# An own list scheduler for two interleaved attention layers: order, buffers and copying engine set by a planned-time simulation

## The chip, the cores and the metric

The kernel runs on one core of a Trainium2 chip. The core has five engines that matter here: PE (TensorE, matrix products; its weight loads are listed apart as PEld), DVE (VectorE), ACT (ScalarE), POOL (GpSimd) and SP (SyncE, which here only issues DMAs). Each executes its own list of instructions strictly in the order in which they stand in it, and waits on semaphores for the others. The metric is the time of one execution on the device, in microseconds (us); the lower the better.

## What is computed

Four residual layers over a sequence of 2048 rows of 576 numbers: A, B, A, B, with the same weights in both turns.

```
x = x + A(layernorm(x));  x = x + B(layernorm(x))     (twice)

A: q, k, v of 32 heads x 18; each position attends to itself and 7 earlier ones,
   2 apart (8 logits, softmax); output projection
B: for each segment of 32 rows, in order:
     h = [mem (8 rows), segment (32 rows)]
     q, k, v = h Wq, h Wk, h Wv            32 heads x 128
     p = softmax(mask(q k^T / sqrt(128)))  40 x 40 per head
     o = (p v) Wo;  mem = o[0:8];  output rows = o[8:40]
```

In B the memory of a segment is computed from the one before: 64 segments that follow one another, twice. A is local.

## The kernel before

All values are kept transposed, features on the 128 partitions (576 is 4.5 blocks of 128). Matrix operands are bf16, sums are f32 in PSUM, which has eight banks: three single ones in rotation (`ps_r`), one tile of four banks (`ps_o`), one for the output projection (`ps_y`).

Both B layers run together: a step t handles segment t of layer 2 (lane 0) and segment t - 6 of layer 4 (lane 1), 80 columns in all: twice 32 rows and twice 8 rows of memory. There are 64 + 6 = 70 steps. `b_step` (L638) issues a step:

- `qk` (L441, 11 groups of three heads): 30 matmuls of 80 columns into one bank, then one copy to `b_qk`, in turn by ACT (L459) and DVE (L461).
- `vpass` (L470): three passes of two halves, 20 matmuls each, for the rows of lane 0, of the memory, and of lane 1. Copies by ACT (L487) or DVE (L489) as written in the step.
- `score_m`, `score_x`: the logits of the memory rows and of the segment rows, for 16 heads at a time (r = 0, 1). `softmax` (L492): maximum, subtraction (DVE), exp (ACT), sum, reciprocal (DVE), multiplication by DVE for the memory rows (`em`) and by POOL for the segment rows (`ex`, L503); DVE transposes both (L521, L543).
- `pv_m` (L545, per r): the memory rows' product with V into the four-bank tile, copied to `OT` by DVE (L560). `pv_x` (L563): the segment rows' product, copied to `OT` by ACT and DVE in turn (L588, L590).
- `oproj` (L593): 160 matmuls into `b_psY`; it needs the memory columns of `OT` from this step and the segment columns from the step before. `mem_out` (L604): three DVE copies put the new memory into the next step's input `hT` (L616 to L618). With these the next step's q, k and v can start.

The A layers go in tiles of 64 rows (32 tiles a layer), `a_tile` (L247): layer norm, q, k, v from 15 weight blocks that SP streams from DRAM through six buffers (`a_w`, L242), products q*k on POOL (`a_big`, L310), logits by a matmul, softmax, spreading back into the four-bank tile (`a_psB`), copies to `a_big` by ACT and DVE in turn (L350, L352), multiplication with v on DVE (L363), three reductions on POOL (L364, L365, L367), output projection from five more blocks, second layer norm. The last 14 columns of k and v go to the next tile through `a_halo` by DVE copies (L284, L285, L299, L300). `finish_out` (L396) adds the last layer and writes the output.

What sets the order: the step's instructions are issued at high priority in the order written in `b_step`; the tiles are generators, which `fill` (L662) advances by a planned amount of PE time after each block. `chain` fixes the order of the matmul blocks on PE. The other engines' order is set by a scheduler from priorities.

## Time and profile before

| | us |
|---|---|
| median of 3 runs | 3577.89 (3569.14 to 3592.28) |
| profiled execution, own time | 3581.54 |
| its span, first to last instruction | 3579.8 |
| PE busy | 2646.4 (74%) |
| DVE busy | 1583.8 (44%) |
| ACT busy | 1051.7 (29%) |
| POOL busy | 1007.2 (28%) |
| mean granted clock of PE | 0.880 |

Busy time is that in which at least one instruction of the engine was at work. The granted clock says at what share of its full speed PE was allowed to run. In the groups of instructions a row gives line, engine, operation, tiles and count, then busy time and the mean of one in ns, then the engine's idle time just before them with what ended it. In a timeline a row begins with start and length in us, and has in brackets how long the engine had been idle and what released it. In the windows, a row is: stretch, length, then busy time and count for PE, PEld, DVE, ACT, POOL, then granted clock, DMA share and GB/s.

### The profile page before, as it was taken

The numbers are of one execution on the slowest core, as the hardware profiler recorded it, in microseconds if no ns is written. First come the engines' busy times: TensorE is split into PE (matmuls) and PEld (weight loads), VectorE is DVE, ScalarE is ACT, GpSimd is POOL, SyncE is SP. The second block draws the span as 40 slices with busy tenths as digits, with TensorE's granted clock in tenths as the row PEclk, the third lists the DMA queues.
The fourth block names the chain that finished last, engine by engine and source line by source line (L and its number), as shares of the span: only waits on it lengthen the run. The fifth ranks groups of instructions, "written<-read, shape, count | busy, mean of one in ns | idle before, by whom it ended". The sixth has DMA issues, their size and how long they took to land. (4 is left out here: it accounts for less than half of the span.)

```text
span 3579.8 us, 159066 instructions
## 1 busy us (share of the span) xinstructions
PE 2646.4 (74%) x73360; PEld 2213.0 (62%) x73360; DVE 1583.8 (44%) x3949; ACT 1051.7 (29%) x2317; POOL 1007.2 (28%) x1007
## 2 busy tenths in 40 slices
PE   0577777777768868777786786777688687778888
PEld 0466666666656646665665665666566466657667
DVE  1344444444444434443453454444445344444443
ACT  0233232232323323322332332333233233222232
POOL 3233323323232322323323332233323323221210
PEclk9998889898979879897897988989899799978899
DMA  9233223232232323223332332333323333222210
GB/s 288 76 85 88 77 78 84 80 97 70 83 84 74 97 84 93 80 85 88 85 99 66 89 95 68 98 88 86 85 73 97 91 86 84 82 68 59 56 40 12
DMA packets 368640, 304.06 MB, mean 85 GB/s; under 512 B 146788, under 2 KB 364452, under 8 KB 366436
## 3 DMA queue, kind: packets, MB, share of 16 engines
q1 hardware_dynamic: 364724, 275.02, 27.7%
q0 software_dynamic: 3248, 18.88, 1.5%
q8 instruction: 573, 9.39, 1.1%
q14 instruction: 95, 0.78, 0.1%
HBM read 260.88 MB, written 32.90 MB: 82 GB/s over the span
## 5 line engine op out<-in xcount | busy, mean ns | idle before, releaser
L452 PE MATMUL b_psqk<-hT,wq 128*128 128x80 bf16 x8960 | 729.9, 209 | 171.6 <-DVE b_qk L461 69.0
L452 PE MATMUL b_psqk<-hT,wk 128*128 128x80 bf16 x8960 | 729.0, 209 | 0.0
L601 PE MATMUL b_psY<-OT,wo 128*128 128x80 bf16 (+1 forms) x11360 | 551.8, 222 | 182.0 <-DVE OT L560 181.2
L601 PEld LDWEIGHTS <-wo 128*128 128x128 bf16 x11360 | 532.6, 114 | 187.8 <-issue 185.0
L452 PEld LDWEIGHTS <-wq 128*128 128x128 bf16 x8960 | 506.9, 104 | 213.2 <-issue 194.5
L484 PE MATMUL b_psv<-wv,hT 128*32 128x512 bf16 x6720 | 476.1, 405 | 43.7 <-DVE b_qk L461 31.3
L452 PEld LDWEIGHTS <-wk 128*128 128x128 bf16 x8960 | 496.1, 105 | 0.2 <-issue 0.2
L454 PE MATMUL b_psqk<-hT,wq_r 128*128 128x80 bf16 x2240 | 467.5, 209 | 0.1
L454 PE MATMUL b_psqk<-hT,wk_r 128*128 128x80 bf16 x2240 | 467.0, 208 | 0.0
L484 PEld LDWEIGHTS <-hT 128*32 128x32 bf16 x8400 | 219.6, 101 | 271.8 <-issue 98.6
L503 POOL TENSOR_TENSOR ex<-ex,b_sumx 128x384 bf16<-128x384 bf16 x140 | 116.6, 833 | 936.0 <-DVE b_sumx L502 595.1
L459 ACT CAST b_qk<-b_psqk 128x480 bf16<-128x480 f32 (+1 forms) x420 | 223.9, 534 | 491.7 <-PE b_psqk L454 489.7
L310 POOL TENSOR_TENSOR a_big<-a_q,a_k 128x1024 bf16<-128x1024 bf16 (+1 forms) x192 | 320.1, 1692 | 134.6 <-ACT a_k L296 132.8
L290 PE MATMUL a_psqkv<-a_xn,a_w 128*128 128x64 bf16 x4800 | 260.9, 202 | 130.4 <-DMA a_w<-wA_blk 111.5
L461 DVE CAST b_qk<-b_psqk 128x480 bf16<-128x480 f32 x350 | 224.7, 646 | 209.2 <-PE b_psqk L454 207.0
L364 POOL TENSOR_TENSOR a_big<-a_big 128x1280 bf16<-128x1280 bf16 x64 | 166.7, 2605 | 513.3 <-DVE a_big L363 513.3
L290 PEld LDWEIGHTS <-a_w 128*128 128x128 bf16 x4800 | 195.6, 103 | 186.2 <-DMA a_w<-wA_blk 138.7
L487 ACT CAST V<-b_psv 128x512 bf16<-128x512 f32 x350 | 200.9, 588 | 180.7 <-PE b_psv L484 180.3
L454 PEld LDWEIGHTS <-wq_r 128*128 128x128 bf16 x2240 | 234.4, 105 | 0.0
L454 PEld LDWEIGHTS <-wk_r 128*128 128x128 bf16 x2240 | 234.0, 104 | 0.0
L390 POOL TENSOR_TENSOR xnb<-xres,ln_st 128x256 bf16<-128x256 f32 (+1 forms) x128 | 65.7, 533 | 454.8 <-DVE ln_st L232 454.8
L484 PE MATMUL b_psv<-wv_r,hT 128*32 128x512 bf16 x1680 | 175.7, 401 | 2.2 <-issue 2.2
(139 smaller groups left out, 3586.0 us busy)
## 6 DMA issues: line engine op xcount, KB each, us to landing
a_w<-wA_blk SPq DMA_DIRECT2D x1280, 160.0 KB, 3.1
x1T<-xres SPq DMA_DIRECT2D x32, 160.0 KB, 2.8
xres<-x1T SPq DMA_DIRECT2D x32, 160.0 KB, 2.5
d2T<-b_stg SPq DMA_DIRECT2D x64, 80.0 KB, 1.9
dl<-d2T SPq DMA_DIRECT2D x32, 160.0 KB, 2.3
x3T<-xres SPq DMA_DIRECT2D x32, 160.0 KB, 3.1
d4T<-b_stg SPq DMA_DIRECT2D x64, 80.0 KB, 2.4
xres<-x3T SPq DMA_DIRECT2D x32, 160.0 KB, 2.7
```

The source lines that it names most:

```text
L290: mm = [nc.tensor.matmul(ps[:, c, :], lhsT=w[:, kc, :], rhs=xn[:, kc, :], start=(kc == 0), stop=(kc == 4)) for kc in range(5)]
L310: nc.gpsimd.tensor_tensor(out=big[:, c0:c0 + nb], in0=qT[:, c0:c0 + nb].unsqueeze(2).to_broadcast([P, nb, AW, T]), in1=win(kT, c0, nb), op ...
L364: nc.gpsimd.tensor_tensor(out=big[:, :, 0:4], in0=big[:, :, 0:4], in1=big[:, :, 4:8], op=ALU.add)
L390: nc.gpsimd.tensor_tensor(out=o, in0=i, in1=bc(m), op=ALU.subtract)
L452: mm.append(nc.tensor.matmul(ps[:, hh, wi, :], lhsT=wt[:, kc, h * P:(h + 1) * P], rhs=hT[:, kc, 0:W80], start=(kc == 0), stop=False))
L454: mm.append(nc.tensor.matmul(ps[:, hh, wi, :], lhsT=wr[:, (h % 16) * P:(h % 16 + 1) * P], rhs=hT[:, 4 + h // 16, 0:W80], start=False, stop ...
L459: nc.scalar.copy(out=sb[:, 0:n], in_=ps[:, 0:n])
L461: nc.vector.tensor_copy(out=sb[:, 0:n], in_=ps[:, 0:n])
L484: mm.append(nc.tensor.matmul(ps[c * 32:(c + 1) * 32, :], lhsT=l, rhs=w, start=(kc == 0), stop=(kc == 4)))
L487: nc.scalar.copy(out=o, in_=ps[:])
L503: eng.tensor_tensor(out=e, in0=e, in1=ss[:].unsqueeze(len(shp) - 1).to_broadcast(shp), op=ALU.mult)
L601: mm.append(nc.tensor.matmul(self.psY[:, mb, c0:], lhsT=self.wo[:, w0:w0 + P], rhs=self.OT[:, h, c0:], start=(h == 0 and mb == 0), stop=(h ...
```

## The change

All arithmetic stays, and so do matmuls, tilings, the sizes and counts of the buffers (but for one `fin` instead of two, and four instead of three of the small softmax sums), the two lanes and their distance of 6 steps, and the setup. What changes is who decides the order. The program is now first written down as a graph of operations (`_Op`), each with the engine or the engines that may do it, its planned length, a priority (a time in steps), the operations that it depends on, and the buffers that it takes and uses. `_Plan.run` then plays it through in planned time: whenever an engine is free, it takes the ready operation with the lowest priority number whose buffers are free, emits its instructions at once, and frees buffers when the last user is done. So the order of instructions on each of the five engines, the buffer, and the engine for each copy that ACT and DVE can both do come out of this play. The order is emitted as it is (`manual_schedule`). Semaphores are set from the data's dependencies, as before.

Beside this: all PSUM banks in rotation, and all other buffers, are plain tiles handed out by the plan; the halo copies are POOL's; the three reductions can be POOL's or DVE's (`PD`); the copies of q, k, v, `OT`, `big` and of the layer norms' inputs can be ACT's or DVE's (`AD_`); the squares can be DVE's; the projection is cut into eight pieces that other work can come between; V's two halves and both scores are single operations. ACT's copies are written as an activation with scale 1.

The diff, cut to its core:

```diff
+    LAT = {"PE": 0.22, "DVE": 0.1, "ACT": 0.1, "POOL": 0.12, "SP": 2.4, "NONE": 0.0}
+    SWITCH = 0.1
...
+    def run(self, log=None):
+        ready = {e: [] for e in self.LAT}
...
+                for e, heap in ready.items():
+                    if free[e] > now + 1e-9:
+                        continue
+                    skipped = []
+                    pick = None
+                    while heap:
+                        it = heapq.heappop(heap)
+                        o = it[2]
+                        if o.done:
+                            continue
+                        need = {}
+                        for b in o.acq:
+                            need[b.pool] = need.get(b.pool, 0) + 1
+                        if all(len(self.pools[p]) >= k for p, k in need.items()):
+                            pick = o
+                            break
+                        skipped.append(it)
+                    for it in skipped:
+                        heapq.heappush(heap, it)
+                    if pick is None:
+                        continue
+                    o = pick
+                    o.done = True
+                    for b in o.acq:
+                        b.t = self.pools[b.pool].pop(0)
+                    us = o.us[o.eng.index(e)]
+                    if e == "PE":
+                        if o.mode != mode:
+                            us += self.SWITCH
+                            mode = o.mode
+                    if o.fn is not None:
+                        o.fn(e)
+                    busy[e] += us
+                    if log is not None:
+                        log.append((now, us, e, o))
+                    free[e] = now + us
...
+                elif what == "done":
+                    for b in o.uses:
+                        b.left -= 1
+                        if b.left == 0:
+                            self.pools[b.pool].append(b.t)
+                    for s in o.next:
+                        s.wait -= 1
+                        if s.wait == 0:
+                            enable(s, now)
+        return now, busy
...
+def _act(n):
+    return 0.22 + 0.00072 * n
+def _dve(n):
+    return 0.15 + 0.00105 * n
+def _evac(n):
+    return (_act(n), _dve(n))
+AD_ = ("ACT", "DVE")
...
+                    def hcopy(e, part=part):
+                        h = dst[part].t[:, :, 0:HALO]
+                        if first:
+                            nc.gpsimd.memset(h, 0.0)
+                        else:
+                            nc.gpsimd.tensor_copy(out=h, in_=hin[0].t[:, part - 1])
+                    got[part, "h"] = pl.op("POOL", 0.25, hcopy, pr(0.22), [o] if first else [o, hin[1]],
+                                           uses=[dst[part]] if first else [dst[part], hin[0]])
...
+            evs.append(pl.op(AD_, _evac(512),
+                             lambda e, g=g, ps=ps: self.copy(e, big.t[:, 0:4, :, g * 16:(g + 1) * 16],
+                                                             ps.t[:, g, :].rearrange("p (c w t) -> p c w t", c=4, w=AW)),
+                             pr(0.56), [b], uses=[ps, big]))
...
+        PD = ("POOL", "DVE")
+        o = pl.op(PD, (2.6, 0.85), lambda e: self.tt(e, big.t[:, :, 0:4], big.t[:, :, 0:4], big.t[:, :, 4:8], ALU.add),
+                  pr(0.64), mus, uses=[big])
+        o = pl.op(PD, (1.44, 0.5), lambda e: self.tt(e, big.t[:, :, 0:2], big.t[:, :, 0:2], big.t[:, :, 2:4], ALU.add),
+                  pr(0.66), [o], uses=[big])
+        o = o_o = pl.op(PD, (0.78, 0.33), lambda e: self.tt(e, oT.t[:], big.t[:, :, 0], big.t[:, :, 1], ALU.add),
+                        pr(0.68), [o], acq=[oT], uses=[big])
...
+        if r == 0:
+            self.OTm = pl.buf("OTm")
+            self.om_ev = [pl.op(AD_, (0.4, 0.41), lambda e: self.copy(e, o_, ps.t[:, :, 0:64].rearrange("p c (i q) -> p c i q", i=4)),
+                                prio, [o], acq=[self.OTm], uses=[ps])]
+        else:
+            self.om_ev.append(pl.op(AD_, (0.4, 0.41), lambda e: self.copy(e, o_, ps.t[:, :, 0:64].rearrange("p c (i q) -> p c i q", i=4)),
+                                    prio, [o, self.om_ev[0]], uses=[ps, self.OTm]))
...
+        gate = pl.op("NONE", 0.0, None, prio, [o], acq=[OTx])
+        self.OTx = OTx
+        self.ox_ev = []
...
+            self.ox_ev.append(pl.op(AD_, _evac(512), ev, prio, [gate], uses=[ps, OTx]))
...
     def b_step(self, t):
-        self.qkt, self.PTm, newPTx = {}, {}, {}
-        last = t == self.nsteps - 1
-        self.PTx = newPTx
-        seq = []
+        self.qkt, self.qk_ev, self.PT = {}, {}, {}
+        if t == 0:
+            self.vpass(t, 2, 0.0)
         for g in range(11):
-            seq.append((self.qk, t, g))
-            if g == 9:
-                seq.append((self.load_x, t + 1))
-            if g == 6:
-                seq += [(self.vpass, t, 1, ("act", "dve")), (self.score_m, 0), (self.score_x, 0)]
-        seq += [(self.vpass, t, 0, ("act", "act")), (self.score_m, 1), (self.score_x, 1), (self.pv_m, 0),
-                (self.oproj, 0, 12), (self.pv_m, 1), (self.oproj, 12, 16), (self.oproj, 16, 24), (self.oproj, 24, 32),
-                (self.mem_out, t), (self.x_out, t - 1), (self.pv_x,)]
-        if not last:
-            seq.append((self.vpass, t + 1, 2, ("act", "act")))
-        for fn, *args in seq:
-            c0 = self.clk
-            with self.hp():
-                fn(*args)
-            if self.clk > c0:
-                self.fill(SHARE * (self.clk - c0))
...
+            self.qk(t, g, t + 0.05 + 0.045 * g)
+        self.vpass(t, 1, t + 0.36)
+        self.vpass(t, 0, t + 0.54)
+        self.scores(t, 0, "m", t + 0.30)
+        self.scores(t, 0, "x", t + 0.32)
+        self.scores(t, 1, "m", t + 0.51)
+        self.scores(t, 1, "x", t + 0.57)
+        self.pv_m(t, 0, t + 0.60)
+        self.pv_m(t, 1, t + 0.62)
+        dep = self.oproj(t, [t + 0.63 + 0.02 * k for k in range(8)])
+        if t + 1 < self.nsteps:
+            self.load_x(t + 1)
+        self.mem_out(t, dep, t + 0.8)
+        self.x_out(t - 1, dep, t + 0.9)
+        self.pv_x(t, t + 0.92)
+        if t + 1 < self.nsteps:
+            self.vpass(t + 1, 2, t + 0.95)
...
+        with self.tc.manual_schedule():
+            self.setup()
+            self.trace()
...
+        end, busy = pl.run(LOG)
```

PE has the same 73,360 matmuls in the built program. Three places show how the order moves.

DVE before, around the second memory copy to `OT` of a step (L560; `b_ptx` is the transposed `ex`, which POOL multiplies first; L284 and L285 are halo copies):

```order
L560 CAST OT<-b_psom 128x16x16
L503 TENSOR_TENSOR em_262<-em_262,b_summ 128x4x80
L501 TENSOR_REDUCE b_sumx<-ex_264 128x8
L521 STREAM_TRANSPOSE b_ptm<-em_262 128x384
L502 RECIPROCAL b_sumx<-b_sumx 128x8
L285 COPY a_v<-a_halo_47653 128x5x14
L543 STREAM_TRANSPOSE b_ptx<-ex_264 128x512
L284 COPY a_k<-a_halo_47653 128x5x14
L560 CAST OT<-b_psom 128x16x16
L616 CAST hT_259<-b_psY 128x4x16
```

ACT after, at the same place of a step (`xs` is the layer norm's input, `big` and `ex` as before, the copies of 128x16x16 to `OT` are the memory copies, `o` is the four-bank tile):

```order
L223 ACTIVATE xT_303<-r_342 128x320
L223 ACTIVATE big_319<-o_343 128x4x8x16
L673 ACTIVATE ex_273<-r_340 128x8x48
L223 ACTIVATE xs_308<-xT_303 128x5x64
L223 ACTIVATE OT<-o_343 128x16x16
L394 ACTIVATE xs_308<-xT_303 128x5x64
L223 ACTIVATE OT<-o_343 128x16x16
L223 ACTIVATE stg_293<-psY 128x5x2x32
```

The memory copies have moved from DVE, where the transpose of `ex` and the halo stood ahead of them, to ACT, where a copy of `big`, an exp and a layer norm's input stand ahead.

POOL before, around the multiplication of `ex` (L503): reductions of one tile, products of the next.

```order
L364 TENSOR_TENSOR a_big<-a_big 128x5x256
L365 TENSOR_TENSOR a_big<-a_big 128x5x128
L367 TENSOR_TENSOR a_o<-a_big 128x320
L310 TENSOR_TENSOR a_big<-a_q,a_k 128x1024 x2
L503 TENSOR_TENSOR ex_264<-ex_264,b_sumx 128x8x48
L310 TENSOR_TENSOR a_big<-a_q,a_k 128x512
```

POOL after, at a comparable place (L489, L504 and L505 are halo copies, the 128x1024 and 128x512 rows the products):

```order
L489 COPY kT_312<-halo_315 128x5x14
L230 TENSOR_TENSOR big_319<-qT_311,kT_312 128x1024
L489 COPY vT_314<-halo_315 128x5x14
L230 TENSOR_TENSOR big_319<-qT_311,kT_312 128x1024
L230 TENSOR_TENSOR ex_272<-ex_272,sum_299 128x8x48
L504 COPY halo_316<-kT_312 128x70
L505 COPY halo_316<-vT_314 128x70
L230 TENSOR_TENSOR big_319<-qT_311,kT_312 128x512
```

The reductions no longer stand there (DVE has them in this tile), the halo copies do, and two of the three products still stand ahead of `ex`.

DVE before, where a step ends (new memory to `hT`, segment copies to `OT`):

```order
L616 CAST hT_259<-b_psY 128x4x16
L617 CAST hT_259<-b_psY 64x16
L618 CAST hT_259<-b_psY 64x16
L590 CAST OT<-b_psox 128x2x4x64 x2
L376 TENSOR_TENSOR xres<-xres,a_psY 128x320
L461 CAST b_qk<-b_psqk 128x480
```

DVE after, where a step ends:

```order
L893 CAST hT_264<-psY 128x4x16
L894 CAST hT_264<-psY 64x16
L895 CAST hT_264<-psY 64x16
L225 CAST OT<-o_343 128x2x4x64 x2
L225 CAST V_278<-r_342 128x512
L225 CAST V_278<-r_341 128x512
L225 CAST qk_282<-r_342 128x480
L225 CAST qk_283<-r_341 128x480
L225 CAST qk_284<-r_340 128x480
```

Behind the copies to `OT` there now stand both halves of a V pass, which ACT had before, and three of the next step's q and k copies; the banks are named `r`.

More of the change, by code (lines that the diff above doesn't have):

```diff
@@ L1 @@
+import heapq
 from contextlib import ExitStack
@@ L286, in a_tile @@
+        got = {}
         for part in (0, 1, 2):
[L287 removed]
+            ps = pl.buf("r")
+            o = o_n
             for c in range(5):
[L289 to L297 removed]
```

1003 lines of the change are left out of this document (539 added, 464 removed).

## The prediction

> **What bounds the kernel now.** I read first the page's head and the busy time of five stretches (before the first matmul, the first tile, the first step, the 68 steps from the first memory copy to the last, the tail).
>
> ```profile
> span 3579.8 us, 159066 instructions
> PE 2646.4 (74%) x73360; PEld 2213.0 (62%) x73360; DVE 1583.8 (44%) x3949; ACT 1051.7 (29%) x2317; POOL 1007.2 (28%) x1007
> ```
> ```profile
> 0.00:92.80 92.80, 0.01 (x1) 0.04 (x2) 10.43 (x31) 1.28 (x1) 32.15 (x97) 1.00 0.90 279
> 92.80:132.40 39.60, 15.25 (x201) 9.89 (x202) 7.43 (x24) 8.83 (x21) 13.35 (x12) 1.00 0.33 96
> 132.40:172.20 39.80, 33.66 (x890) 29.52 (x893) 17.01 (x46) 10.43 (x24) 10.03 (x9) 0.87 0.23 67
> 172.20:3530.30 3358.10, 2560.89 (x71132) 2141.85 (x71128) 1531.28 (x3812) 1018.64 (x2245) 950.05 (x887) 0.88 0.29 81
> 3530.30:3579.80 49.50, 36.57 (x1170) 31.66 (x1158) 17.67 (x39) 12.56 (x26) 1.66 (x2) 0.90 0.07 18
> ```
> ```profile
> L616 DVE CAST hT<-b_psY x69: 180/225/226, 172.2 to 3530.3; 128x64 bf16<-128x64 f32 x57, 128x32 bf16<-128x32 f32 x12
> ```
>
> The last row is the copy of the new memory into the next step's input, once a step, the recurrence. From 172.2 to 3530.3 are 68 steps, (3530.3 - 172.2) / 68 = 49.4 us each. In one, PE is busy 2560.89 / 68 = 37.7 us and idle 11.7; DVE is busy 22.5, ACT 15.0, POOL 14.0. So no engine is full: PE is the nearest to a bound and loses a quarter of each step to waits. The sum is made against the profiled run (span 3579.8, own time 3581.5); the median of the runs shown, 3577.9, is 0.1% from it.
>
> Then PE's groups with what ended their idle time, and one place in the timeline, on PE, POOL and DVE.
>
> ```profile
> L601 PE MATMUL b_psY<-OT,wo 128*128 128x80 bf16 (+1 forms) x11360 | 551.8, 222 | 182.0 <-DVE OT L560 181.2 <-ACT OT L588 0.7
> L452 PE MATMUL b_psqk<-hT,wq 128*128 128x80 bf16 x8960 | 729.9, 209 | 171.6 <-DVE b_qk L461 69.0 <-ACT em L499 34.0 <-ACT b_qk L459 16.7
> L290 PE MATMUL a_psqkv<-a_xn,a_w 128*128 128x64 bf16 x4800 | 260.9, 202 | 130.4 <-DMA a_w<-wA_blk 111.5 <-POOL a_xn L271 10.0 <-ACT em L499 2.9
> L339 PE MATMUL a_psB<-a_e,epadT 32*128 32x128 bf16 x1280 | 44.4, 235 | 119.3 <-DVE a_e L330 44.6 <-DVE a_big L352 41.8 <-DVE OT L590 31.9
> ```
> ```profile
> 2038.00 4.16 PE L601 MATMUL b_psY<-OT,wo 128*128 128x80 bf16 x60 [2.28 <-DVE OT L560]
> 2047.21 4.61 PE L601 MATMUL b_psY<-OT,wo 128*128 128x80 bf16 x80 [3.15 <-DVE OT L560]
> ```
> ```profile
> 2035.70 2.60 POOL L364 TENSOR_TENSOR a_big<-a_big 128x1280 bf16<-128x1280 bf16 x1 [5.67 <-DVE a_big L363]
> ...
> 2040.85 3.92 POOL L310 TENSOR_TENSOR a_big<-a_q,a_k 128x1024 bf16<-128x1024 bf16 x2
> 2044.73 0.82 POOL L503 TENSOR_TENSOR ex<-ex,b_sumx 128x384 bf16<-128x384 bf16 x1
> ```
> ```profile
> 2045.59 0.71 DVE L543 STREAM_TRANSPOSE b_ptx<-ex 128x512 bf16<-128x512 bf16 x1 [5.85 <-POOL ex L503]
> ...
> 2046.74 0.41 DVE L560 CAST OT<-b_psom 128x256 bf16<-128x256 f32 x1
> ```
>
> The waits are not missing work but an order in in-order queues. At 2047.21 the output projection (psY) has waited 3.15 us for a copy of 0.41 us (OT, the memory rows of the attention output). That copy stood on DVE behind a transpose that waited 5.85 us for POOL's ex multiply, and this stood on POOL behind 9 us of the layer-A tile's reductions and products. Over the run this one wait is 181.2 us on PE; the weight ring (a_w) is 111.5, the bank copies of q and k 69.0, the four-bank tile (a_psB) 119.3 from several sides.
>
> The clock adds to it:
>
> ```profile
> 2044.50:2046.00 1.50, 0.00 (x0) 0.00 (x0) 0.41 (x1) 0.00 (x0) 1.50 (x3) 1.00 0.00 0
> ...
> 2047.50:2049.00 1.50, 1.50 (x27) 1.50 (x25) 0.00 (x0) 0.00 (x0) 0.00 (x0) 0.50 0.04 11
> 2049.00:2050.50 1.50, 1.50 (x26) 1.50 (x24) 0.00 (x0) 0.00 (x0) 0.00 (x0) 0.50 0.00 0
> 2050.50:2052.00 1.50, 1.50 (x68) 1.44 (x66) 0.15 (x2) 0.00 (x0) 0.00 (x0) 0.90 0.00 0
> ```
>
> After 3.15 us of idle the granted clock is 0.50 for 3.4 us, and the 80 projection matmuls take 4.61 us. The clock of the 68 steps is 0.88; if it is always 1 or 0.5, 24% of the time is at half. PE does about 0.24 x 37.7 = 9.0 us of a step then, of which half, 4.5 us, is surcharge. So PE's work at full clock is 37.7 - 4.5 = 33.2 us a step, and the 49.4 are 33.2 work, 4.5 clock, 11.7 idle.
>
> The Trainium skill (TensorE: Matmul & The Clock Gate, Part 1) has the clock go to half after an idle window of about 3.4 us and back after a busy one, and this place agrees. The same part says that for modelling, the penalty is under 1% of a typical span: by that the clock would be worth under 36 us here, and the sum below would lose its clock term and come out about 250 us higher. The rows above speak for 4.5 us a step, 68 x 4.5 = 306 us, and I go by the rows.
>
> **The change part by part.**
> PE issues the same matmuls in the same shapes, so the 33.2 us stay. A matmul is recorded about 0.17 us past its successor's start, and each wait that I count from the last issue counts this tail again; with five gaps a step I take 0.9 off: 32.3.
>
> Setup, the first tile and the first step are chains of single operations; the SP queue has the same weight loads ahead of the first x. I leave them at 172.2 us. The tail (49.5) follows the step's speed, 42.
>
> Moved to other queues: the memory copy of OT from DVE to ACT nearly always; the halo copies from DVE to POOL, 0.2 us each and nothing behind them on PE; about half of the tile's reductions from POOL to DVE. POOL's 14.0 us a step leave room. DVE takes the reductions, some squares and more evacuations and gives up the OT and halo copies; an estimate from the entries of its new order at its rows' means is 26 us a step, two thirds of 39, so it doesn't bound. The wait of 181.2 us goes, as at the three places shown DVE no longer stands between POOL and the projection.
>
> What is late next I worked out by walking two steps of the new order (a period: one layer-1 and one layer-3 tile) with these durations:
>
> ```profile
> 112.92 0.69 DVE L352 CAST a_big<-a_psB 128x512 bf16<-128x512 f32 x1 [1.39 <-ACT a_big L350]
> 113.64 0.59 ACT L350 CAST a_big<-a_psB 128x512 bf16<-128x512 f32 x1 [0.76 <-DVE a_big L352]
> ```
> ```profile
> L588 ACT CAST OT<-b_psox 128x512 bf16<-128x512 f32 x140 | 81.9, 585 | 71.0 <-DVE OT L590 52.8 <-PE b_psox L581 17.4
> L350 ACT CAST a_big<-a_psB 128x512 bf16<-128x512 f32 x128 | 74.9, 585 | 85.4 <-DVE a_big L352 43.8 <-PE a_psB L339 40.8
> L357 ACT CAST a_big<-a_psB 128x512 bf16<-128x512 f32 x64 | 37.7, 589 | 61.6 <-PE a_psB L339 60.8
> L499 ACT ACTIVATE em<-b_psm 128x320 bf16<-128x320 f32 x140 | 61.2, 437 | 262.5 <-DVE b_psm L498 227.3 <-PE b_psom L556 16.8 <-PE b_psx L537 15.3
> L222 ACT ACTIVATE ln_xs<-xres 128x320 bf16<-128x320 f32 x128 | 59.5, 465 | 0.0
> ```
> ```profile
> L590 DVE CAST OT<-b_psox 128x512 bf16<-128x512 f32 x140 | 96.7, 691 | 100.0 <-ACT OT L588 99.6
> L352 DVE CAST a_big<-a_psB 128x512 bf16<-128x512 f32 x128 | 88.2, 689 | 91.0 <-ACT a_big L350 89.0
> L489 DVE CAST V<-b_psv 128x512 bf16<-128x512 f32 x70 | 48.3, 689 | 105.3 <-PE b_psv L484 105.1
> L560 DVE CAST OT<-b_psom 128x256 bf16<-128x256 f32 x140 | 56.4, 403 | 28.1 <-PE b_psom L556 27.9
> L498 DVE TENSOR_TENSOR b_psm<-b_psm,b_nmxm 128x320 f32<-128x320 f32 x140 | 69.7, 498 | 10.4 <-DVE b_nmxm L497 0.9
> L497 DVE TENSOR_REDUCE b_nmxm<-b_psm 128x4 f32<-128x320 f32 x140 | 68.1, 486 | 107.2 <-PE b_psm L516 106.9
> ```
> ```profile
> 2053.69 1.04 PE L484 MATMUL b_psv<-wv,hT 128*32 128x512 bf16 x16
> 2056.15 0.31 PE L452 MATMUL b_psqk<-hT,wk 128*128 128x80 bf16 x4
> 2056.33 0.31 PE L452 MATMUL b_psqk<-hT,wq 128*128 128x80 bf16 x4
> ```
>
> The first fence shows what the planner doesn't know: pieces of one tile copied by ACT and DVE in turn run one after the other (DVE waited 1.39 us for ACT, then ACT 0.76 for DVE), while the plan has them side by side. Covers come from the last fence: five q/k matmuls in 0.18 us, a V half (20 matmuls) in 1.1. I add 0.1 to 0.3 us for handing on from engine to engine, the more where PE's pipeline has to drain first.
>
> Turn of the steps: four OT copies one after the other, 2 x 0.585 + 2 x 0.691 = 2.55, then on DVE the V copy, 0.69, makes 3.2; the first q/k group, which needs V's bank, is covered by two V halves and 20 tile matmuls (an estimate of 0.6 at the same pace), 2.8. With 0.5 for handing on, the chain ends 3.7 us after the last product: gap 0.9. At the other turn of the period ACT has the squares and copies of two layer norms ahead of OT (4 x 0.465): gaps 1.2 and 1.5. Together 3.6.
>
> Scores: a bank is held for 0.486 + 0.498 + 0.437 + 0.5 for handing on = 1.9 by max, add and exp; what PE has meanwhile (the x scores and 20 tile matmuls) is about 1.1: gap 0.8. At the period's three other places, with what stands ahead on DVE, 0.65, 0.4 and 0.5. Together 2.35.
>
> The four-bank tile o4, of which there is one: big's copies 2 x 0.585 + 2 x 0.689 + 0.3 = 2.85 behind 60 q/k matmuls (2.15), gap 0.8; at the second tile of the period DVE has max and add first, gap 1.3; then the first memory product waits for the last copy (0.589 + 0.3), 0.9, and the second for the first one's copy, 0.403 plus half an ACT entry, 0.9. Together 3.9.
>
> Sum 9.85 per period, 5.0 us a step (before 11.7). Bounds: 2, if the copies do run side by side and the score gaps alone stay; 11.7, if the queues block as before.
>
> Clock: only the last three gaps of o4 stand close together, about 3 us in 5; one half-clock window of 3.4 us in two steps costs 1.7, so 0.85 a step (bounds 0 and the 4.5 of now). Ring: the same 20 blocks a tile through six buffers, but the matmuls that use them are spread over the step; now 111.5 / 70 = 1.6 us a step, I take half, 0.8 (bounds 0 and 1.6).
>
> Step: 32.3 + 5.0 + 0.85 + 0.8 = 39.0. Time: 172 + 68 x 39.0 + 42 = 2866, about **2860 us**.
>
> **The rivals.**
> The plan holds almost as laid, and PE is the bound: gaps 2 us, no half clock, ring hidden, 33.2 + 2 = 35.2 a step; 172 + 68 x 35.2 + 40 = 2600. For it: the instruction costs in the planner are close to the rows (a 512-column copy 0.59 on ACT and 0.69 on DVE). Against it: the serial copies.
>
> The clock's surcharge stays. If the 37.7 us that PE is busy are its work whatever the gaps do, or half-clock windows come as often as now, the step is 37.7 - 0.9 + 5.0 + 0.8 = 42.6, and the time 172 + 68 x 42.6 + 45 = 3110. Against it: each slow stretch looked at follows a gap of over 2 us, and the walk has few of these. The Trainium skill's "<1%" (TensorE: Matmul & The Clock Gate, Part 1), read as no gain from the clock, would lead here.
>
> Drift: an order fixed from planned times has no way to react, so where DMA or DVE run late, the wait comes back elsewhere. With 8.5 idle, the ring's 1.6 and half of today's clock surcharge, 32.3 + 8.5 + 1.6 + 2.3 = 44.7; 172 + 68 x 44.7 + 45 = 3260. For it: DVE rises from 46% of these steps to two thirds, and queues that are fuller hand lateness on. Against it: the longest block, POOL's, is cut up.
>
> Slower: the block moves instead of going. DVE still holds the transpose of ex, which waits for POOL, and the evacuations for PE stand behind it. POOL's products (2 us each) stand ahead of ex in the new order too. If both transposes of a step met the 5.85 us of the place above, a step would gain 11.7 us: 39.0 + 11.7 = 50.7; 172 + 68 x 50.7 + 50 = 3670. It decides from 10.4 us a step. Against it: in the walk POOL is done with ex before DVE comes to the transpose, in all four cases of the period.
>
> No difference: the gains would have to be eaten to the microsecond; I see no mechanism.
>
> **How the numbers follow.** The sum as worked out (2700 to 3050 by the bounds of its terms taken half way): 0.52. PE-bound: 0.24. Surcharge stays: 0.05. Drift: 0.12. Slower: 0.05. Same: 0.02. The range reaches from just under the PE-bound case, 2580, over the surcharge case into the drift case, 3150, and leaves about a tenth at each side. About 1% is what a measurement of this kernel can tell from no change. Faster by over 1%: 0.52 + 0.24 + 0.05 + 0.12 = 0.93; within 1% 0.02; slower 0.05.
>
> **What would show it.** Right: the memory copies about 39 us apart; psY no longer waiting for OT on DVE; PE idle 6 us a step, ended mostly by OT, big and V copies; mean clock 0.95 or more; DVE near 65%. The serial copies show as DVE waiting for ACT on OT and big. Wrong: a clock still under 0.9 means gaps still pile up; PE ended by the ring means the DMA term; DVE idle before the transpose of ex by several us means the third rival; idle under 3 us a step means that the walk's gaps were hidden.

## The result and the profile after

The changed kernel takes 2841.76 us (median of 4 runs, 2832.22 to 2859.22) against 3583.54 us before (4 runs): 0.7939 of the time, 95% interval 0.7891 to 0.7987. The forecast was 2860. The profiled execution took 2859.22 us; it is the longest of the four, 17 us above the median, so what is read from it may be some 0.26 us a step too long.

The head of the page after, then the windows of the same five stretches (before the first matmul, first tile, first step, the 68 steps between the first and the last memory copy, tail), then the memory copy's row:

```profile
span 2857.4 us, 159357 instructions
...
PE 2451.8 (86%) x73360; PEld 2021.4 (71%) x73360; DVE 1839.1 (64%) x3981; ACT 977.9 (34%) x2165; POOL 882.5 (31%) x1122
```
```profile
0.00:103.20 103.20, 0.00 (x0) 0.01 (x1) 9.62 (x30) 1.28 (x1) 33.14 (x94) 1.00 0.77 241
103.20:151.00 47.80, 24.14 (x350) 19.31 (x351) 20.36 (x49) 6.25 (x17) 18.82 (x25) 1.00 0.58 169
151.00:191.10 40.10, 34.33 (x987) 27.98 (x989) 27.12 (x51) 13.16 (x28) 11.73 (x15) 0.91 0.27 74
191.10:2811.30 2620.20, 2358.27 (x70871) 1943.99 (x70867) 1759.91 (x3807) 947.70 (x2099) 817.12 (x986) 0.96 0.37 102
2811.30:2857.40 46.10, 35.09 (x1170) 30.07 (x1170) 22.07 (x45) 9.52 (x20) 1.66 (x2) 0.94 0.10 26
```
```profile
L893 DVE CAST hT<-psY x69: 190/225/226, 191.1 to 2811.3; 128x64 bf16<-128x64 f32 x57, 128x32 bf16<-128x32 f32 x12
```

A step is 2620.20 / 68 = 38.53 us (before 49.38). PE is busy 34.68 us of it and idle 3.85 (before 37.66 and 11.72). Busy time times clock is PE's work at full speed: 34.68 x 0.96 = 33.3 us, before 37.66 x 0.88 = 33.1. So the work has not changed. Of the 10.85 us that a step lost, 7.9 are idle time, and 3.1 are the clock's surcharge (4.5 before, 34.68 - 33.29 = 1.4 now). The clock is read to two decimals, so the split is good to about 0.2 us. (Counted in the trace's clock record, which knows only 1 and 0.5, PE's work under the half clock gives 1.6 us a step of surcharge now and 4.5 before.)

The largest of PE's waits over the run after that for the first x, and then DVE's for ACT and POOL (us in total, times, longest):

```profile
PE r L479 <- DMA ring<-wA_blk: 83.1, 85, 2.9
PE o L850 <- issue: 26.1, 21, 2.2
PE o L817 <- ACT big L223: 24.3, 29, 1.4
PE o L552 <- ACT big L223: 23.8, 27, 1.1
PE o L552 <- DVE big L225: 18.9, 32, 2.7
PE r L728 <- DVE V L225: 17.3, 35, 0.7
PE o L817 <- ACT OT L223: 13.8, 26, 0.5
PE r L728 <- ACT qk L223: 9.9, 26, 0.4
...
PE psY L874 <- ACT OT L223: 6.7, 10, 1.0
```
```profile
DVE OT L225 <- ACT OT L223: 76.8, 71, 1.5
DVE big L225 <- ACT big L223: 33.2, 69, 1.2
DVE ptx L691 <- POOL ex L230: 16.4, 45, 0.6
```

The projection's (psY) wait of 181.2 us for a copy on DVE is gone, and DVE's wait for POOL's ex (ptx) fell from 171.0 to 16.4 us. The weight ring leads now, and then the four-bank tile o: its rows that are ended by copies of big and OT make 24.3 + 23.8 + 18.9 + 13.8 = 80.8 us. The serial copies that the prediction spoke of stand in the second list: DVE waits 76.8 and 33.2 us for ACT within OT and big.

One place shows what such waits do to the clock. PE's timeline, and windows of 3.4 us beside it:

```profile
1502.02 0.24 PE L552 MATMUL o<-e,epadT 32*128 32x128 bf16 x4 [0.90 <-ACT big L223]
1503.04 0.51 PE L817 MATMUL o<-ptm,V 32*128 32x16 bf16 x48 [0.78 <-ACT big L223]
1504.07 0.53 PE L817 MATMUL o<-ptm,V 32*128 32x16 bf16 x48 [0.53 <-ACT OT L223]
1504.53 4.65 PE L874 MATMUL psY<-OT,wo 128*128 128x80 bf16 x93
```
```profile
1500.20:1503.60 3.40, 1.63 (x77) 1.38 (x77) 3.30 (x9) 3.12 (x7) 0.00 (x0) 1.00 0.54 152
1503.60:1507.00 3.40, 2.93 (x86) 2.90 (x86) 3.15 (x6) 1.16 (x4) 2.17 (x2) 0.50 0.39 115
1507.00:1510.40 3.40, 3.40 (x98) 3.40 (x96) 0.81 (x2) 0.00 (x0) 1.53 (x1) 1.00 0.15 53
```

These are the prediction's three gaps of the four-bank tile, in its order; the first two are near the sizes that it gave (0.8 or 1.3, then 0.9), the third is 0.53 where it had 0.9. None is over 0.90 us, but the first two lie in one window of 3.40 us, in which PE was busy only 1.63, and the next window ran at half the clock. The Trainium skill (TensorE: Matmul & The Clock Gate, Why this matters for your kernels) advises no idle gaps over some 3 us; here a sum of short ones did it, and the measurement decides.

It isn't a single case. Between the first and the last memory copy the clock record has 64 windows at half clock, in 61 places. In the window ahead of them the most idle time was ended by the ring in 27 places, by copies of big or OT in 27, and in 7 by nothing that the profile shows. In 24 of the 61 no single gap there reached 1 us.

### The profile page after: what moved, and what is told of

Its sections match the earlier page's. It is cut to its first block, busy times and chain, and to the rows that moved or that the text cites. A ratio compares the mean times of both kernels' runs of the same rounds, so it can differ in the third digit from the quotient of the medians.

```text
span 2857.4 us, 159357 instructions
## 1 busy us (share of the span) xinstructions
PE 2451.8 (86%) x73360; PEld 2021.4 (71%) x73360; DVE 1839.1 (64%) x3981; ACT 977.9 (34%) x2165; POOL 882.5 (31%) x1122
## 4 chain that ended last, share of the span: by engine, by line
PE 58%; DVE 15%; DMA 10%; ACT 9%; issue 4%; SPq 3%; POOL 1%; ACTq 0%; DVEq 0%; POOLq 0%
PE r L728 17%; PE psY L874 14%; PE r L759 12%; DMA ring<-wA_blk 10%; PE r L479 5%; PE r L730 4%; DVE big L230 4%; ACT big L223 3%; DVE big L225 2%; SPq L300 2%; DVE OT L225 2%; ACT OT L223 2%; PE o L817 2%; PE o L850 1%; DVE r L671 1%
## 5 line engine op out<-in xcount | busy, mean ns | idle before, releaser
L728 PE MATMUL r<-hT,wq 128*128 128x80 bf16 x8960 | 695.0, 202 | 31.3 <-DVE V L225 17.3
L728 PE MATMUL r<-hT,wk 128*128 128x80 bf16 x8960 | 694.1, 202 | 0.0
L728 PEld LDWEIGHTS <-wq 128*128 128x128 bf16 x8960 | 468.1, 100 | 86.5 <-issue 79.3
L759 PE MATMUL r<-wv,hT 128*32 128x512 bf16 x6720 | 481.2, 408 | 12.9 <-ACT em L673 3.4
L874 PE MATMUL psY<-OT,wo 128*128 128x80 bf16 (+1 forms) x11360 | 474.7, 210 | 17.4 <-issue 9.3
L225 DVE CAST qk<-r 128x480 bf16<-128x480 f32 (+1 forms) x465 | 294.1, 632 | 299.3 <-PE r L730 295.1
L728 PEld LDWEIGHTS <-wk 128*128 128x128 bf16 x8960 | 465.4, 100 | 0.0
L730 PE MATMUL r<-hT,wq_r 128*128 128x80 bf16 x2240 | 452.6, 202 | 1.8 <-issue 1.8
L730 PE MATMUL r<-hT,wk_r 128*128 128x80 bf16 x2240 | 452.9, 202 | 0.0
L230 POOL TENSOR_TENSOR big<-qT,kT 128x1024 bf16<-128x1024 bf16 (+1 forms) x192 | 329.0, 1722 | 152.6 <-ACT kT L223 143.9
L479 PE MATMUL r<-xn,ring 128*128 128x64 bf16 x4800 | 236.2, 198 | 99.1 <-DMA ring<-wA_blk 83.1
L479 PEld LDWEIGHTS <-ring 128*128 128x128 bf16 x4800 | 179.0, 100 | 162.4 <-DMA ring<-wA_blk 108.9
L225 DVE CAST OT<-o 128x512 bf16<-128x512 f32 x138 | 95.2, 691 | 161.3 <-ACT OT L223 76.8
L223 ACT ACTIVATE OT<-o 128x256 bf16<-128x256 f32 (+1 forms) x282 | 131.1, 490 | 165.2 <-DVE OT L225 97.4
```

The costliest lines, as they stand in the source:

```text
L223: nc.scalar.activation(out=out, in_=in_, func=ACT.Copy, scale=1.0 if scale is None else scale)
L225: (nc.vector if e == "DVE" else nc.gpsimd).tensor_copy(out=out, in_=in_)
L230: (self.nc.vector if e == "DVE" else self.nc.gpsimd).tensor_tensor(out=out, in0=in0, in1=in1, op=op)
L479: nc.tensor.matmul(ps.t[:, c * T:(c + 1) * T], lhsT=w.t[:, kc, :], rhs=xn.t[:, kc, :], start=(kc == 0), stop=(kc == 4))
L728: nc.tensor.matmul(pv[:, hh, wi, :], lhsT=wt[:, kc, h * P:(h + 1) * P], rhs=hT.t[:, kc, 0:W80], start=(kc == 0), stop=False)
L730: nc.tensor.matmul(pv[:, hh, wi, :], lhsT=wr[:, (h % 16) * P:(h % 16 + 1) * P], rhs=hT.t[:, 4 + h // 16, 0:W80], start=False, stop=True)
```

## The experiments

Theory A: a few operations stood in the wrong queue (OT's memory copy and the halo copies on DVE). Theory B: the order of all queues made the gain. The first two runs tell them apart.

**The kernel before with the two kinds of copies moved.**

```diff
-        nc.vector.tensor_copy(out=hk[:, 0], in_=kT[:, :, T:T + HALO])
+        nc.gpsimd.tensor_copy(out=hk[:, 0], in_=kT[:, :, T:T + HALO])
...
-        nc.vector.tensor_copy(out=o, in_=ps[:, :, 0, 0:64].rearrange("p c (i q) -> p c i q", i=4))
+        nc.scalar.copy(out=o, in_=ps[:, :, 0, 0:64].rearrange("p c (i q) -> p c i q", i=4))
```

> The kernel before with two things moved and nothing planned: the four halo copies of a tile from DVE to POOL, and the memory copies to OT from DVE to ACT. Theory A (the gain is the unblocking of DVE behind POOL): the 181 us of the projection waiting for OT go, with their share of the clock's surcharge (181/797 of 306, 70 us) and some of the other DVE waits; 3250 to 3350 us. Theory B (the gain is the order of all queues together): PE waits for the next late thing instead; 3480 us or more.

3336.31 us, ratio 0.9329 (0.9303 to 0.9354). The time lies in the range set for theory A, 3250 to 3350; but what theory A was priced at there is only a third of the gain. PE's waits, from this run's trace:

```profile
PE b_psY L601 <- ACT OT L560: 76.0, 83, 1.7
PE a_psY L373 <- POOL a_o L367: 57.7, 9, 6.4
PE a_psB L339 <- DVE a_e L330: 43.8, 17, 4.9
```

The wait for OT shrank from 181.2 to 76.0 us, and waits behind POOL's and DVE's other blocks remain. DVE's waits for POOL, in the kernel before (first two rows) and in this run (last row):

```profile
DVE a_k L284 <- POOL a_big L310: 221.3, 55, 9.3
DVE b_ptx L543 <- POOL ex L503: 171.0, 131, 5.9
DVE b_ptx L543 <- POOL ex L503: 199.9, 133, 6.1
```

So before, DVE stood still longest not for ex but at a halo copy behind POOL's products, which the prediction had priced at the copy's own 0.2 us. The move takes this wait from DVE; the one for ex stays.

**The changed kernel with each copy, reduction and halo nailed to the engine it had before.** The plan decides order and buffers alone.

```diff
-        e4 = pl.op(AD_, _evac(512),
+        e4 = pl.op("ACT", _act(512),
...
-        PD = ("POOL", "DVE")
+        PD = "POOL"
```

> The changed kernel, but each copy, reduction and halo is nailed to the engine that had it before (OT memory copies and halos on DVE, reductions on POOL, ACT and DVE in turn for q and k, and so on); the plan still sets the order and the buffers. Theory A: the block of DVE behind POOL comes back; 3200 us or more. Theory B: most of the gain is kept; 2850 to 3000 us.

2945.46 us, ratio 0.8245 (0.8222 to 0.8268): 638 of the 742 us. B holds: the order makes most of the gain, though both kinds of copies are back on DVE, while A alone makes a third of it. The largest of DVE's waits for POOL that was left:

```profile
DVE ptx L691 <- POOL ex L230: 9.6, 45, 0.4
```

No halo copy waits for POOL's products any more. What came with the plan beside the order (buffers handed out as they come free, the projection in eight pieces) is in this run too and isn't told apart from the order. The free choice of engine goes with the 104 us that are left; how much of these is a plan's luck, see below.

**Destinations of the copies disjoint** (big cut by block, OT by half and heads), against theory C, that the serial copies of the one four-bank tile hold PE.

```diff
-                             lambda e, g=g, ps=ps: self.copy(e, big.t[:, 0:4, :, g * 16:(g + 1) * 16],
+                             lambda e, g=g, ps=ps: self.copy(e, big.t[:, g].rearrange("p w (q t) -> p q w t", q=NQ),
...
-                self.copy(e, self.OT[:].rearrange("p (r c i) q -> p r c i q", r=2, c=4)[:, :, c, :, 16:W80],
+                self.copy(e, self.OT[:, 16 * r + 8 * h:16 * r + 8 * h + 8, 16:W80].rearrange("p (c i) k -> p c i k", c=2),
```

> The changed kernel, with the same four copies of the four-bank tile to big and to OT cut along the destination's outer dimension, so that each writes a stretch of its own: same sizes, same engines to choose from. Theory C (the gaps at the four-bank tile come from copies that ACT and DVE must do one after the other): DVE and ACT no longer wait for each other on big and OT, the waits of PE for big and OT (80 us and 14 us) fall to under half, the clock rises to about 0.97; 2740 to 2790 us. Rival D (the copies come late because their queues are full): within 25 us of the changed kernel, 2842.

2838.65 us, ratio 0.7937 (0.792 to 0.7954): no change. Each copy now also reads two or four of the banks, and the copies stay serial:

```profile
DVE OT L225 <- ACT OT L223: 75.9, 71, 1.2
DVE big L225 <- ACT big L223: 33.4, 69, 1.2
```

So overlapping destinations aren't what orders them; what the serial copies cost PE, this run can't say.

**The four-bank tile made of two tiles of two banks**, one copied by ACT, one by DVE.

```diff
-        self.pl.pool("o4", [pp.tile([P, 4, 512], F32, name="o4")])
+        self.pl.pool("o4", [[pp.tile([P, 2, 512], F32, name=f"o4{h}") for h in "ab"]])
...
-            self.ox_ev.append(pl.op(AD_, _evac(512), ev,
+            self.ox_ev.append(pl.op(AD_[c // 2], _evac(512)[c // 2], ev,
```

> The four-bank tile o4 is made of two tiles of two banks; ACT copies one, DVE the other, so neither waits for the other (the copies over all four banks become two of half the size). Theory C, the serial copies of o4 hold PE: DVE's waits for ACT on OT and big (76.8 and 33.2 us in the changed kernel) fall below 15 us together, PE's waits for copies of big and OT (some 81 us) below 45, the clock rises to 0.97, and the time is 2770 to 2810 us. Rival, PE would wait there anyway for what comes next (V, scores, the ring): the copies overlap but the idle time only changes its name, 2825 to 2860 us.

2840.03 us, ratio 0.7925 (0.7891 to 0.7959). DVE has no wait for ACT on OT or big any more, though the four copies write what they wrote in the changed kernel, so what was ordered is two engines' reads of one PSUM tile, even of different banks of it. The time is still the same, in the range of the rival: o4's waits for copies of big and OT fell to 47.5 us, others came up.

```profile
PE r L479 <- DMA ring<-wA_blk: 50.8, 72, 2.5
PE o4b L552 <- DVE OT L225: 32.9, 29, 2.8
PE r L728 <- DVE qk L225: 31.0, 27, 2.6
PE r L402 <- ACT xs L394: 30.3, 26, 1.2
```

The edit also changed the plan (the ring's wait fell to 50.8 us with no buffer added), so this alone doesn't say what C is worth.

**The planner is told that the copies are serial.** The chip's work stays.

```diff
-                             pr(0.56), [b], uses=[ps, big]))
+                             pr(0.56), [b, *evs[-1:]], uses=[ps, big]))
...
-            self.ox_ev.append(pl.op(AD_, _evac(512), ev, prio, [gate], uses=[ps, OTx]))
+            self.ox_ev.append(pl.op(AD_, _evac(512), ev, prio, [gate, *self.ox_ev[-1:]], uses=[ps, OTx]))
```

> The planner is told that the four copies of big and the four of OT follow one another (each depends on the one before); the chip's work stays the same. If the o4 gaps come from the plan not knowing it, other work now stands in PE's queue there: PE's waits for big and OT fall from some 81 us to under 50, time 2780 to 2820 us. If there is no other work to put there (one o4 tile, its users next in line), the waits stay above 70 us and the time is 2825 to 2870 us.

2807.52 us, ratio 0.7822 (0.7777 to 0.7867), 34 us less, as if the plan's ignorance had cost that. But PE's waits for copies of big and OT at the four-bank tile are 66.0 us (80.8 in the changed kernel), between the under 50 and the over 70 of the two expectations, and one of them grew (`o L552 <- DVE big`, from 18.9 to 54.0 us).

**One duration for all operations of an engine.**

```diff
-        o.us = (us,) * len(o.eng) if isinstance(us, (int, float)) else tuple(us)
+        o.us = tuple(MEAN[e] for e in o.eng)
```

> In the planner every operation of an engine lasts the mean of that engine (PE 0.583, DVE 0.70, ACT 0.517, POOL 1.19, SP 0.428 us); priorities, buffers, dependencies and the latencies stay. Theory D, the durations make the order good: PE's idle time returns to 7 us a step or more, clock under 0.93, time 3050 us or more. Rival P, the priorities and the choice among what is ready do most, and the durations only trim: under 2950 us.

3092.01 us, ratio 0.8633 (0.8597 to 0.8668), 250 us more, with the clock at 0.93. Theory D holds in part (idle time 6.1 us a step, where 7 or more was expected): priorities and readiness with wrong durations still keep 492 of the 742 us, and the right durations make the last third. The ring's wait doubled:

```profile
PE r L482 <- DMA ring<-wA_blk: 164.0, 185, 3.1
PE o L820 <- DVE ptm L694: 49.1, 63, 2.0
```

**Seven ring buffers, and then with the order held.** The first lets the planner use the seventh, too; the second lets it have only six in use, and PE, DVE, ACT and POOL then have the changed kernel's order to the row.

```diff
-        tiles("ring", 6, [P, 5, P])
+        tiles("ring", 7, [P, 5, P])
```

> The changed kernel with seven weight buffers in the ring instead of six. Theory E (the 83 us of waits for ring are too few buffers for the 3.1 us of landing): the wait falls to about half, with one throttled window less in two periods; 2780 to 2820 us. Rival F (SP issues late, behind other entries of its queue): within 15 us of 2842, wait for ring over 70 us.

2786.13 us, ratio 0.7792 (0.7765 to 0.7818), in theory E's range, though the ring wait fell from 83.1 to 53.5 us only, not to half. With the order held, one more line:

```diff
-                        if all(len(self.pools[p]) >= k for p, k in need.items()):
+                        if all(len(self.pools[p]) >= k + (p == "ring") for p, k in need.items()):
```

> Seven ring buffers on the chip, but the planner may have only six in use, so that the order on PE, DVE and ACT is that of the changed kernel to the row. If the gain of the seventh buffer is the chip's (a weight load no longer waits for the oldest buffer), the ring wait on PE falls from 83 to about 55 us and the time is 2780 to 2815 us. If the gain came from the order that a planner with seven buffers finds, the ring wait stays near 83 us and the time at 2830 to 2855 us.

2828.49 us, ratio 0.7909 (0.7889 to 0.7929), whose interval overlaps the changed kernel's. PE's ring wait:

```profile
PE r L479 <- DMA ring<-wA_blk: 71.5, 78, 2.6
```

That is 11.6 us less than 83.1, and the time 13 us less, which the intervals don't tell from nothing. The other 42 us of the run before came from the order that the planner found with seven. Neither expectation fits fully; the reading "the chip's gain" falls for the larger part.

**A nudge of the plan as a control.**

```diff
-    LAT = {"PE": 0.22, "DVE": 0.1, "ACT": 0.1, "POOL": 0.12, "SP": 2.4, "NONE": 0.0}
+    LAT = {"PE": 0.22, "DVE": 0.11, "ACT": 0.1, "POOL": 0.12, "SP": 2.4, "NONE": 0.0}
```

> Control: only one number of the planner is nudged (it reckons 0.11 us instead of 0.10 from a DVE operation's end to the next engine's start); the kernel's work is the same and about an eighth of PE's rows stand elsewhere. If single plans differ by luck as much as the ring and the serial copies moved the time, this comes out 30 us or more away from 2842; if those two moves mean something, it stays within 15 us, 2827 to 2857.

2787.37 us, ratio 0.7798 (0.7775 to 0.7822): 54 us less for 0.01 us in a table. So one plan can differ from the next by as much as the ring (56) or the serial chain (34) seemed to give. It is one nudge; how far plans spread wasn't measured. Its steps:

```profile
187.70:2738.20 2550.50, 2305.23 (x70881) 1913.73 (x70885) 1779.81 (x3832) 928.65 (x2073) 809.90 (x988) 0.98 0.37 105
```

A step is 37.51 us, with 3.61 idle and 33.90 busy: of the 1.02 us gained between the profiled executions (73 us apart, the medians 54), 0.24 are idle time and 0.78 are clock. The same step of the sequence as at 1502 above, in this run's timeline of PE:

```profile
1460.17 0.40 PE L552 MATMUL o<-e,epadT 32*128 32x128 bf16 x16 [0.21 <-ACT OT L223]
1460.51 1.61 PE L874 MATMUL psY<-OT,wo 128*128 128x80 bf16 x40
1461.95 0.90 PE L587 MATMUL r<-oT,ring 128*128 128x64 bf16 x25
1462.68 0.88 PE L874 MATMUL psY<-OT,wo 128*128 128x80 bf16 x20
1463.49 0.23 PE L552 MATMUL o<-e,epadT 32*128 32x128 bf16 x4
...
1464.78 0.51 PE L817 MATMUL o<-ptm,V 32*128 32x16 bf16 x48
1465.82 3.03 PE L874 MATMUL psY<-OT,wo 128*128 128x80 bf16 x80 [0.53 <-ACT OT L223]
```

The pieces of the projection (psY) now stand between the users of the four-bank tile. Of the three gaps one is left, with a new one of 0.21, and the 80 matmuls after it take 3.03 us at full clock, where 93 took 4.65. Over the run PE's waits at the four-bank tile for copies of big and OT fell from 80.8 to 32.3 us, and the windows at half clock between the first and the last memory copy from 64 to 26; in 2 places instead of 27 they follow such copies. The copies are as serial as before (ACT waits 100.0 us for DVE within OT, 97.4 in the changed kernel); PE has something to do meanwhile.

**Two combinations.** The first: seven ring buffers, two tiles for o4, and in the setup the weight-block stores ahead of the output weights' loads:

```diff
+            for i in range(WOB):
+                part, c = divmod(i, 5)
+                col0 = part * D + HPC * AD * c
+                nc.sync.dma_start(out=self.wA[i], in_=wn[:, :, col0:col0 + P])
             won = tp.tile([P, 5, 640], BF16, name="c_wo")
```

> Seven ring buffers, o4 in two tiles, and in the setup the stores of the q/k/v weight blocks ahead of the loads of the output weights. The first matmul starts at about 93 us instead of 103.2. If the three gains add up: 2842 less 56 (ring), 40 (o4) and 10 (start), some 2735 us, range 2715 to 2755. Rival, the ring's and o4's gaps partly stand in for one another and the clock windows they cause are shared: 2760 to 2786 us.

2815.48 us, ratio 0.7854 (0.7817 to 0.7891). Both expected ranges are missed. The gains don't add; that most of them were the plans' own is the likely reason, which this run alone doesn't show. The start didn't move either (first matmul at 102.6 us): not the stores' place held it, but DVE, whose clears end at 23.85 us; the first store goes out at 23.87. In the changed kernel's timeline, DVE's clears of the weight padding, for which the stores wait, and SP's stores:

```profile
22.55 0.19 DVE L287 MEMSET c_wqkv<- 128x160 uint32 x1
22.99 0.81 DVE L288 MEMSET c_wqkv<- 64x896 uint32 x1 [0.25 <-DVE c_wqkv L287]
```
```profile
24.67 64.08 SPq L300 DMA_DIRECT2D wA_blk<-c_wqkv  x15
```

Before, the two clears ran at 0.92 and 1.35. Now every queue has the setup's own written order, in which they stand behind the mask constants that wait for POOL. The second combination moves them up, with seven ring buffers, the stores early, and the serial chain:

```diff
+            nc.vector.memset(wn[:, :, 1728:1792], 0.0)
+            nc.vector.memset(wn[64:128, 4, :], 0.0)
             tmp = tp.tile([P, P], F32, name="c_tmp")
```

> Three edits together: seven ring buffers, the copies of big and OT serial in the plan, and in the setup the two clears of the weight padding at the head of DVE's queue and the weight-block stores ahead of the output weights' loads. The first matmul starts at about 92 us (103.2 in the changed kernel), as DVE's clears no longer stand behind the masks. If the gains add up: 2842 less 56, 34 and 11, some 2741 us, 2725 to 2757. Rival, ring and o4 gaps stand in for one another: 2760 to 2780 us.

2755.1 us, ratio 0.7708 (0.769 to 0.7726), the best of all: 87 us under the changed kernel, and in the range for gains that add up. The clears ran at 0.92 and 1.36, the stores from 9.70, the first matmul at 91.4 instead of 103.2, the first memory copy at 176.7 instead of 191.1. The 12 us of the first matmul are the edit's; the rest comes with a step of 37.25 us, only 0.26 from the nudged 37.51, so that the time doesn't show that the other gains add.

**An eighth ring buffer**, with the room taken from other buffers: the run before, with three counts changed, and the output written from the input's tile (`x0`).

```diff
-        tiles("nmx", 4, [P, 8], F32)
-        tiles("sum", 4, [P, 8], F32)
+        tiles("nmx", 3, [P, 8], F32)
+        tiles("sum", 2, [P, 8], F32)
...
-        tiles("ot", 1, [P, D])
-        tiles("ring", 7, [P, 5, P])
+        tiles("ring", 8, [P, 5, P])
```

> As the run before with an eighth ring buffer (room for it from sharing the input tile with the output tile, three instead of four buffers of row maxima and two instead of four of row sums). If buffers are still what the ring waits for, its wait on PE falls by another 10 to 20 us and the time by 15 to 25 us against that run; if the shared tiles or the DMA's own time hold it now, the time stays within 10 us of that run or rises.

3041.58 us, ratio 0.8514 (0.8492 to 0.8536): 286 us more. PE's ring wait is 71.6 us (43.0 in the run before), and new waits are up:

```profile
PE r L527 <- POOL big L230: 48.0, 20, 5.2
PE o L551 <- DVE e L544: 33.4, 21, 3.1
```

Which of the buffers that lost room did it stays open.

Steps of some of the runs, from the windows between the first and the last memory copy:

| | us a step | PE busy | PE idle | clock | busy x clock |
|---|---|---|---|---|---|
| before | 49.38 | 37.66 | 11.72 | 0.88 | 33.1 |
| two copies moved | 45.63 | 36.08 | 9.55 | 0.92 | 33.2 |
| one duration | 41.92 | 35.84 | 6.08 | 0.93 | 33.3 |
| engines fixed | 39.69 | 34.82 | 4.87 | 0.96 | 33.4 |
| changed kernel | 38.53 | 34.68 | 3.85 | 0.96 | 33.3 |
| nudged | 37.51 | 33.90 | 3.61 | 0.98 | 33.2 |
| best | 37.25 | 34.07 | 3.19 | 0.97 | 33.0 |

In the runs that aren't in the table the product is 33.1 to 33.4, but for 32.5 with eight ring buffers, where PE is idle for 45% of the time at half clock. Where PE's busy time is taken at the clock of its own moment, its work is 33.0 to 33.4 in all runs.

## Why the prediction was right, and where it wasn't

The cause was right in kind: same work, an order that lets the small operations through, and with the gaps also most of the clock's surcharge gone. What was to show it came: memory copies 38.53 us apart (39), psY no longer behind DVE, a clock of 0.96, DVE 64% busy, DVE waiting for ACT on OT and big. Two signs came only in part: PE idles 3.85 us a step instead of 6, and though the copies of OT, big and V end most of it that the list shows (80.8 + 17.3 + 6.7 = 104.8 us), the largest single wait is the ring's, 83.1 us.

The number, 2860, is nearer than its terms, whose errors cancelled by luck; in the order of the list, 68 - 133 + 37 + 19 + 4 is -5 us (the ring is counted with the gaps):

- **Work**, 32.3 forecast, 33.3 measured. The step "each wait that I count from the last issue counts this tail again; with five gaps a step I take 0.9 off" was wrong as a deduction from the work. Busy time times clock stays at 33.0 to 33.4 in the table whatever the idle time is. 68 us too few. Taken off the gaps, where it was argued from, it would have left them nearer, but still too long.
- **Gaps**, 5.0 forecast. Of the walk's three places, o4 took 80.8 / 68 = 1.2 us a step (1.95 forecast). The turn of the steps and the scores were expected at 1.8 and 1.2; of their waits only those of L728 for V and qk, (17.3 + 9.9) / 68 = 0.4, reach the list's upper part. All of PE's idle time, with the ring, is 3.85, where 5.8 was forecast: 133 us too many. That I priced the covers at those two places too low is argued only; no run takes it apart. (In the o4 term 2.85 behind 2.15 is 0.7, not 0.8, which is 0.05 us a step.)
- **Ring**, 0.8 forecast as half of before's, 83.1 / 68 = 1.2 measured. That spreading its matmuls would halve the wait had no row behind it.
- **Clock**, 0.85 forecast as one half-clock window in two steps, from "only the last three gaps of o4 stand close together"; 1.4 measured. The window at 1503.6 is the one foreseen, and of such the run has about as many as forecast, 27 places for 34 windows. The ring's waits, which the term left out, bring another 27, and 7 follow waits on no shown cause (most of them `o L850 <- issue`, 26.1 us in all). 37 us too few.
- **Start**, "I leave them at 172.2 us", 191.1 measured. "The SP queue has the same weight loads ahead of the first x" overlooked that DVE's queue, too, gets the written order. 10 us are the clears, as the best version shows; another 8 are the first tile's chain, 47.8 against 39.6 us, in which PE now does more (350 matmuls against 201). 19 us too few. Tail 42, measured 46.1, 4 us too few.

The rivals: the PE-bound case (2600) wasn't reached by any version, though the nudged plan and the best one went 54 and 87 us of the way. Drift (idle 8.5 a step) and the kept surcharge fell with 3.85 and 0.96. The slower case, DVE held by POOL's ex, fell with 16.4 us.

And the hit is finer than the thing allows: the nudge, which no walk by hand would price, moves the time by 54 us, three times the distance of forecast and measurement (18 us). Of the effects found, only those well over this are settled by one plan each, order against two moved copies and durations, and beside them the start, which is read from the trace itself.

## What to carry to other kernels

Where several in-order queues feed one busy engine, plan the order of all of them from measured durations; moving single operations off a blocked queue gave a third of it here. Judge any edit of a planned kernel against nudged plans, or hold the order fixed, since a nudge of 0.01 us moved the time by 1.9%, and a ring buffer that seemed worth 56 us was worth 13 with the order held, if anything. And put independent pieces between users of a scarce buffer: here short gaps close together cost twice, once idle and once at half clock.

## What the runs showed of the hardware

- PE's clock fell to half after a window of 3.40 us with 1.63 us of work and no gap over 0.90 us, and was back after one window with 2.93 us of work. In the 61 places where it fell between the memory copies, PE was at work for at most 62% of the window ahead.
- The surcharge was 4.5 us a step before, 68 x 4.5 = 306 us of 3580, and 1.4 in the changed kernel, 95 us. The Trainium skill (TensorE: Matmul & The Clock Gate, A second HAM failure mode: psum-queue depth-cycling) tells of a kernel in which PE idles briefly, but so often, that the clock goes up and down; the window at 1500.20 agrees.
- As built here, copies by ACT and DVE from one PSUM tile waited for one another though they read different banks (76.8 and 33.2 us on DVE); with two tiles, one for each engine, these waits were gone.
- PE waited up to 2.2 us at the segment rows' product with V (L850) on nothing that the profile's waits show, 26.1 us in all. The longest, at 835.7 us, stands within the product, after 65 of its 96 matmuls. In the whole run 18 such waits on any line are of 0.9 us or more, and each began 0.3 to 2.3 us after a 16 KB packet of the instruction queue had started, of which there are 573, one in 4.8 us; so the loading of PE's own instructions is a likely cause, which no run tests.
